# A fused attention, gated feed-forward and routed-expert kernel: more weight conversion beside attention, a smaller conversion allowance afterwards

## The chip, the cores and the metric

One core of a Trainium2 chip runs the whole program in one launch. The metric is the device time of one execution in microseconds (us); lower is better. The engines are called PE (TensorE, matrix products), DVE (VectorE), ACT (ScalarE), POOL (GpSimd) and SP (SyncE, which issues nearly all DMAs here). Each engine works through its own instructions in the order in which they were written and waits at semaphores where it needs another engine.

## The reference, cut to what matters

Three layers follow one another on 2304 tokens of width 512:

```python
# 1. attention: batch 4, heads 8, 576 positions, head width 64, window of 64 positions
attn = softmax(mask(q @ k.T / 8));  x = attn @ v            # x: 2304 x 512
# 2. gated feed-forward, width 1536
xn = x / sqrt(mean(x * x) + 1e-6) * rms_g
x2 = (silu(xn @ w_gate) * (xn @ w_val)) @ w_out
# 3. eight experts, width 1024, one for each token
e = argmax(x2 @ wg);  out = prob[e] * (relu(x2 @ w1[e]) @ w2[e])
```

The weights of layer 2 arrive as 64-bit floats and are turned into 32-bit floats on the chip ("conversion"). The products of layers 2 and 3 are each made of three products of split operands: a number is split into a high part h and the rest l, and h·h, h·l and l·h are added.

## The kernel before, in words

**Attention** goes in 48 groups (loop at L499, group g). A group computes scores (PE), softmax (DVE L205, ACT L209), normalisation (DVE L217, POOL L218), transposes (PE L223), their copy out of PSUM (DVE L227), the product with v (PE) and the copy of the result (L245 on ACT or DVE in turn, L246 on ACT). The steps of one group are spread over six passes of the loop: transposes come 4 passes after the scores (LT), the product with v and its output 5 (LV). `guard(g)` (L213) adds 1e-9 to the row sums. Five passes after the last group (g = 48 to 52) drain it, and PE fills them with the first unit of layer 2.

**Side work in attention.** Other work is written as generators that yield a nominal price in us for DVE's time, and `Task` and `beside` (L251 to L285) hand it out. `attending_work(g)` (L468) runs in each pass between `normalise` and `softmax`; it has a credit that grows by CREDIT per pass, is capped at 1.0 and may go negative. It offers, in this order, `early_splits`, `norm(0)` (from pass 17), `norm(1)` (from pass 30) and, until a given number of steps is converted, `conversion`. A task that yields "rest" (it waits for ACT) is passed over until 1.2 of other work is handed out or the call ends; one that yields "step" is passed over until the next call. If all tasks rest, the call ends and what is left of its allowance is lost, but for a carry of at most 0.5 (1.0 in attention, credit and carry together).

**Conversion** of one of the 12 steps (a step is 128 of the 1536 columns) is two halves, each with a load of 768 KB (`w_load`, SP), a Square on ACT (L426) and four DVE instructions (L401, L406, L409, L416) at the nominal prices 0.55, 1.0, 1.0 and 0.9: 6.9 for a step. `norm(i)` normalises a sub-block of 384 tokens: it loads x, squares it (POOL for i < 2, else ACT L329), adds the squares (three DVE adds L334), sums over the partitions with a PE product on a bank lent by the caller, takes 1/sqrt by three Newton steps (ACT L352, DVE L354, DVE L356), and scales and splits (L363, ACT L365, L368). From i = 2 on its prices add up to 10.0: 1.5 for the adds, 0.9 for L344 and L346, 3.6 for Newton, 4.0 for scaling and splitting.

**Layer 2** goes in 72 units (loop at L843). A unit is one step for one sub-block: 24 gate and value products (`gate_val`), then `silu` (ACT L594, DVE L595 and L596, ACT L597, L598), and 9 output products (`out_b`), which PE makes one unit later. Units 0 to 3 are steps 0 and 1 for sub-blocks 0 and 1; units 4 to 23 are steps 2 to 11, each for sub-blocks 0 and 1; block 1 (units 24 to 47) takes sub-blocks 2 and 3 in turn, so that unit 24 needs norm 2 and unit 25 norm 3. In blocks 0 and 1 gate and value products use PSUM banks 0 and 1 in each unit but unit 1, so a unit's first product waits for the L595 of the unit before.

A unit's allowance for side work is `BUDGET[n] + min(spare, 0.5)`, less what splits and evacuations cost (1.2 for the gate and value weights of a step, every second unit); a debt is carried in full. The order is norm 1, conversion, the other norms (`normer`), routing. Two things are forced whatever the allowance: a step is converted three units ahead of its first use (L888), and before the next unit the norm that it needs is finished (L890 to L893):

```python
        budget = BUDGET[n] + min(spare, 0.5)
        budget -= sum(c for c, _ in rest)
        spare = beside([norm1, conv] + bg, budget)          # bg: norm1, normer, routes
        if u + 3 in heads:
            spare -= convert(max(f for _, f, _ in steps[:heads[u + 3] + 1]) + 1, conv)
        if u + 1 < len(units):
            while normed[0] < units[u + 1][1]:
                late = normer if norm1.done else norm1
                late.piece(bk if late.want == "bank" else None)
```

There is one `xr` buffer for all norms from i = 2 on, so norm 3 cannot load before norm 2 has made its last split.

Of the kernel before, what the change touches and what calls it, by code (L numbers as in the profile page):

```python
# [8 lines left out]
F32 = mybir.dt.float32  # L9
# [4 lines left out]
ALU = mybir.AluOpType  # L14
# [12 lines left out]
P = 128  # L27
# [8 lines left out]
SUB = 384  # L36
# [4 lines left out]

LT, LV = 4, 5
NQK = 3
G_LOAD, G_CONV, G_NORM = 8, 14, (12 + LV, 25 + LV)
CREDIT = 0.5, 0.8
BUDGET = [4.8, 3.4, 4.7, 4.7]


@with_exitstack
def attention_moe_moe_kernel(ctx, tc, qT, kT, vw, w1p, rms_g, wg2, wg2T, w2p, out):  # L50
    nc = tc.nc
# [9 lines left out]

    bank = [psum.tile([P, 512], F32, name=f"bank{i}") for i in range(8)]

    for i in range(2):

        nc.vector.memset(bank[i][:, SUB:], 0.0)
    ident = const.tile([P, P], F32, name="ident")
# [35 lines left out]
    wraw_t = [wr_p.tile([P, 2 * WB], F32, name=f"wraw{i}") for i in range(NF // 2)]  # L103
    wraw = [t[:, i * WB:(i + 1) * WB] for t in wraw_t for i in range(2)]
# [24 lines left out]
    wh_t, wl_t = {}, {}  # L129

    def place(k, key, what):

        p = next((p for p in places[key] if p[2] == what), None)
        here = p is not None
        if not here:
            p = min(places[key], key=lambda p: p[3])
        p[2:] = what, k
        wh_t[k, key], wl_t[k, key] = p[:2]
        return here
# [3 lines left out]
    f_p = pool("fill", 1, actx)  # L143
# [17 lines left out]
    a_s = pool("a_s", 3, actx)  # L161

    qz = [f_p.tile([P, P, NBLK], F32, name=f"qz{i}") for i in range(NQK)]
    for q in qz:
        for h in range(2):
            nc.vector.memset(q[64 * h:64 * h + 64, 64 * (1 - h):64 * (1 - h) + 64], 0.0)

    NU = B * NHP
    NG = NU * 3
    q_t, k_t, v_t, xo_t, p_t, pt_t, rs_t = {}, {}, {}, {}, {}, {}, {}  # L170

    def qk_load(u):
        if u < NU:
            b, hp = divmod(u, NHP)
# [10 lines left out]
    def v_load(u):  # L185
        if u < NU:
            b, hp = divmod(u, NHP)
            t, i = (wraw_t[3], u % 4) if u % 4 < 3 else (wraw_t[1], 2)
            v_t[u] = t[:, i * 8 * P:(i + 1) * 8 * P].rearrange("p (w c) -> p w c", c=P)
            nc.sync.dma_start(v_t[u], vw[b, hp])  # L190

    def scores(g):
# [17 lines left out]
                                 accum_out=rs[:, j:j + 1])  # L210

    def guard(g):
        nc.vector.tensor_scalar_add(rs_t[g], rs_t[g], 1e-9)  # L213

    def normalise(g):
        p, rs = p_t[g], rs_t.pop(g)
# [6 lines left out]
            nc.tensor.transpose(bank[3 + g % 2][:, j * P:(j + 1) * P], p[:, j], ident)  # L223

    def pt_copy(g):
        pt = pt_t[g] = wraw_t[1][:, (g % 5) * 3 * P:(g % 5 + 1) * 3 * P]
        nc.vector.tensor_copy(pt, bank[3 + g % 2][:, 0:3 * P])  # L227

    def pv(g):
# [7 lines left out]
    def xo_out(g):  # L237
        u, i0 = g // 3, 3 * (g % 3)
        b, hp = divmod(u, NHP)
        if g % 3 == 0:  # L240
            xo_t[u] = wraw_t[4 + u % 2][:, 4 * 512:4 * 512 + S]
        vb = bank[5 + g % 3][:, 0:3 * P].rearrange("p (j c) -> p j c", j=3)
        xo = xo_t[u]
        x3 = xo.rearrange("p (i c) -> p i c", c=64)
        (nc.scalar.copy if g % 2 else nc.vector.tensor_copy)(x3[0:64, i0:i0 + 3], vb[0:64, :, 0:64])  # L245
        nc.scalar.copy(x3[64:128, i0:i0 + 3], vb[64:128, :, 64:128])  # L246
        if g % 3 == 2:
            nc.sync.dma_start(xdram[b][hp], xo)
# [189 lines left out]
    converted, attending = [0], [True]  # L438
# [14 lines left out]

    def early_splits():

        yield lambda: converted[0] > 0
        place(0, "a", ("b", 0))
        wh, wl = wh_t[0, "a"], wl_t[0, "a"]
        for a in range(0, 1024, 512):
            src, h = wraw[0][:, a:a + 512], slice(a, a + 512)  # L460
            nc.scalar.copy(wh[:, h], src)
            nc.gpsimd.tensor_tensor(out=wl[:, h], in0=src, in1=wh[:, h].bitcast(F32), op=ALU.subtract)
            yield "step"

    conv, early, norm0, norm1, normer = (Task(t) for t in (conversion(), early_splits(), norm(0), norm(1), norms()))
    credit = [0.0]
# [1 line left out]
    def attending_work(g):  # L468
        c = min(credit[0] + CREDIT[g >= G_NORM[1]], 1.0)
        if g >= G_CONV:  # L470
            tasks = [early]
            if g >= G_NORM[0]:
                tasks.append(norm0)
            if g >= G_NORM[1]:
                tasks.append(norm1)
            if converted[0] < 2:
                tasks.append(conv)
            tasks = [t for t in tasks if not t.done]
            c -= on_bank(tasks, bank[(g + 1) % 3 if g < NG else 2])
            c = beside(tasks, c)  # L480
        credit[0] = c
# [100 lines left out]
    def gate_val(u):  # L582
        if u > 0:
            for _ in gate_val_mm(gv_banks(u), *units[u]):
                pass
# [257 lines left out]
    for u, (k, i) in enumerate(units):  # L843
        n = steps[k][0]
        first, last = (i == steps[k][2][x] for x in (0, -1))
        begin = u == starts[blocks[n][2][0]]
        gate_val(u)
        if u == 0:
            beside([norm1, conv], 3.0)
        silu(u)  # L850
        budget = BUDGET[n] + min(spare, 0.5)

        if len(blocks[n][2]) > 1:
            bk = bank[1]
        else:
            bk = bank[4] if n == len(blocks) - 1 else bank[5]
        if u > 0:
            out_b(u - 1)
        if not (begin and len(blocks[n][2]) == 1):
            budget -= on_bank(bg, bk)  # L860
        if u > 0:
            budget -= evac(u - 1)
        if u == stops[i]:
            free[0] = i + 1
        if u in range(2, 2 + 2 * E, 2):

            e = u // 2 - 1
            nc.sync.dma_start(xs[e * NT:e * NT + 4 * P], x2dram[NT:NT + 1].to_broadcast([4 * P, DM]))
        rest = b_split(heads[u + 1], "o") if u + 1 in heads else []
        if u + 2 in heads:  # L870
            rest += b_split(heads[u + 2], "a")
        elif u + 2 >= len(units):
            rest += c_split(u + 2 - len(units), True)
        if conv.done and wg_bc is None:
            right.close()
            g_p, r_p, j_p = (pool(x, b, right, side="right") for x, b in (("g", 1), ("r", 2), ("j", 2)))
            wg_bc = g_p.tile([P, E, DM], F32, name="wg_bc")
            nc.sync.dma_start(wg_bc, wg2T.partition_broadcast(P))
        budget -= sum(c for c, _ in rest)
        spare = beside([norm1, conv] + bg, budget)  # L880
        for _, r in rest:
            r()
        if n == len(blocks) - 1 and last:

            while c_next < NRING and (c_next + 1) * W2B <= (NF + 2 + k - len(steps)) * WB:
                c_load(c_next)
                c_next += 1
# [6 lines that stand above are left out]
        bg = [t for t in bg if not t.done]  # L894
# [178 lines left out]
    with tc.If(n_over > 0):  # L1073
        with tc.For_i(0, n_over, 1) as i:
            ex = nc.values_load(slot[0:1, bass.ds(i, 1)], engines=(ET.SP,), min_val=0, max_val=E - 1)
            row = nc.values_load(slot[0:1, bass.ds(i + NS, 1)], engines=(ET.SP,), min_val=0, max_val=E * NT - 2 * P)
            with tc.tile_pool(name="ovr", bufs=1) as o_p:
                ix = o_p.tile([P, 2, 2], I32, name="oix")
                nc.sync.dma_start(ix, table[bass.ds(row, 2 * P)].rearrange("(j p) w -> p j w", p=P))
                w = o_p.tile([P, NF2, W2B], F32, name="ow")  # L1080
# [4 lines left out]
                for j in range(2):  # L1085
                    nc.gpsimd.indirect_dma_start(
                        out=xg[:, j], out_offset=None, in_=x2dram[:, :],
# [64 lines left out]
```

## Time and profile before

| | |
|---|---|
| timed runs | 901.14 us median of 3 (900.82 to 901.97) |
| the profiled execution | 898.3 us, of which the span from first to last instruction is 896.5 |
| PE, DVE, ACT, POOL busy | 94%, 74%, 46%, 23% of the span |
| mean granted TensorE clock | 0.986 of 2.4 GHz |

Times inside the profile are us from the start of the span. Busy shares are means over stages with different limits: attention lasts until about 130 us, block 0 of layer 2 until about 300, block 1 until about 450. A timeline row has start, duration, engine, line, operation, output and input, how many instructions were merged and, in brackets, the idle time of that engine just before and what ended it. A row of busy time by stretch has the stretch, its length, the busy us (and instructions) of PE, of PE's weight loads, of DVE, ACT and POOL, then PE's granted clock as a share of 2.4 GHz, the DMA engines' busy share and GB/s.

### The profile page before, as it was taken

The numbers are of one execution on the slowest core, as the hardware profiler recorded it, in microseconds if no ns is written. First come the engines' busy times: TensorE is split into PE (matmuls) and PEld (weight loads), VectorE is DVE, ScalarE is ACT, GpSimd is POOL, SyncE is SP. The second block draws the span as 40 slices with busy tenths as digits, with TensorE's granted clock in tenths as the row PEclk, the third lists the DMA queues.
The fourth block names the chain that finished last, engine by engine and source line by source line (L and its number), as shares of the span: only waits on it lengthen the run. The fifth ranks groups of instructions, "written<-read, shape, count | busy, mean of one in ns | idle before, by whom it ended". The sixth has DMA issues, their size and how long they took to land.

```text
span 896.5 us, 13576 instructions
## 1 busy us (share of the span) xinstructions
PE 844.1 (94%) x4667; PEld 774.7 (86%) x4667; DVE 665.6 (74%) x1552; ACT 415.3 (46%) x951; POOL 205.6 (23%) x226
## 2 busy tenths in 40 slices
PE   7999978998999999999999999997999999989995
PEld 7999977887888899999989999986888888878884
DVE  6789979999997677777578985696685765666453
ACT  5777764333443334323233333343564554555352
POOL 3347563323233100001400024003310120121011
PEclk9999998999999999999999999998999999999998
DMA  7988524779742301000120004634385664662010
GB/s 210 296 270 284 166 94 132 222 184 192 220 114 95 106 0 36 1 1 1 60 83 1 1 13 119 256 120 118 105 278 186 215 216 133 210 213 94 3 44 19
DMA packets 47071, 114.49 MB, mean 128 GB/s; under 512 B 10223, under 2 KB 14703, under 8 KB 46834
## 3 DMA queue, kind: packets, MB, share of 16 engines
q1 hardware_dynamic: 42386, 103.50, 38.1%
q0 software_dynamic: 4576, 9.47, 3.1%
q8 instruction: 77, 1.26, 0.6%
q14 instruction: 32, 0.26, 0.1%
HBM read 93.90 MB, written 31.10 MB: 139 GB/s over the span
## 4 chain that ended last, share of the span: by engine, by line
PE 55%; DVE 28%; issue 8%; DMA 4%; ACT 3%; POOL 2%; SPq 0%; DVEq 0%; POOLq 0%; ACTq 0%
PE bank L56 52%; DVE junk L661 4%; DVE wla L552 3%; DMA out_dram<-x,ix 3%; DVE wraw L406 3%; DVE wraw L409 2%; DVE wraw L416 2%; DVE t L596 2%; DVE t L595 2%; DVE wraw L401 2%; PE bank L796 1%; PE bank L223 1%; DVE xt L368 1%; DVE wlo L552 1%; ACT hh L597 1%
## 5 line engine op out<-in xcount | busy, mean ns | idle before, releaser
L56 PE MATMUL bank<-xt,wha 128*128 128x384 f32 (+3 forms) x1728 | 422.6, 329 | 24.6 <-DVE t L595 12.8
L56 PEld LDWEIGHTS bank<-xt,wha 128*128 128x128 f32 x1728 | 305.6, 190 | 43.1 <-DVE t L595 18.2
L56 PE MATMUL bank<-xt,wla 128*128 128x384 f32 (+3 forms) x864 | 282.0, 326 | 3.7 <-POOL wla L552 2.7
L56 PEld LDWEIGHTS bank<-xt,wla 128*128 128x128 f32 x864 | 164.1, 190 | 6.0 <-POOL wla L552 3.0
L56 PE MATMUL bank<-who,hl 128*128 128x512 f32 x384 | 152.5, 397 | 0.6 <-DVE hl L955 0.6
L56 PE MATMUL bank<-wlo,hh 128*128 128x512 f32 x384 | 152.4, 397 | 0.0
L56 PE MATMUL bank<-who,hh 128*128 128x512 f32 x384 | 151.5, 395 | 0.3
L597 ACT CAST hh<-t 128x384 fp32r<-128x384 f32 x72 | 37.0, 513 | 200.6 <-DVE t L596 200.6
L955 DVE SCALAR_TENSOR_TENSOR hl<-bank,hh 128x512 fp32r<-128x512 f32 (+1 forms) x72 | 45.3, 629 | 80.3 <-ACT hh L954 77.2
L552 DVE TENSOR_TENSOR wla<-wraw,wha 128x512 fp32r<-128x512 f32 (+1 forms) x112 | 98.0, 875 | 4.4 <-ACT wha L550 2.8
L56 PEld LDWEIGHTS bank<-who,hl 128*128 128x128 f32 x384 | 72.6, 189 | 17.4 <-DVE hl L955 1.4
L550 ACT CAST wha<-wraw 128x512 fp32r<-128x512 f32 (+1 forms) x113 | 87.1, 771 | 0.0
L954 ACT ACTIVATE hh<-bank 128x512 fp32r<-128x512 f32 (+1 forms) x72 | 39.7, 551 | 99.6 <-PE bank L56 99.3
L971 POOL DMA_INDIRECT out_dram<-x,ix x32 | 34.9, 1091 | 214.3 <-ACT x L970 207.3
L56 PEld LDWEIGHTS bank<-who,hh 128*128 128x128 f32 x384 | 72.8, 190 | 11.8 <-issue 0.5
L56 PEld LDWEIGHTS bank<-wlo,hh 128*128 128x128 f32 x384 | 72.8, 190 | 11.1
L56 PE MATMUL bank<-kt,qz 128*128 128x128 f32 x288 | 76.2, 404 | 5.5 <-DMA kt<-in_kT_dram 4.8
L550 ACT CAST who<-wraw 128x512 fp32r<-128x512 f32 x111 | 68.7, 619 | 21.9 <-PE bank L56 19.6
L56 PEld LDWEIGHTS bank<-kt,qz 128*128 128x128 f32 x288 | 72.3, 333 | 6.1 <-issue 4.8
L552 DVE TENSOR_TENSOR wlo<-wraw,who 128x512 fp32r<-128x512 f32 x99 | 68.1, 688 | 12.4 <-ACT who L550 5.7
L661 DVE SCALAR_TENSOR_TENSOR junk<-x,wg_bc 128x512 f32<-128x512 f32 x120 | 76.1, 687 | 0.0
L209 ACT ACTIVATE wraw<-sm,nm 128x128 f32<-128x128 f32 x144 | 56.2, 391 | 25.9 <-DVE nm L205 25.4
(151 smaller groups left out, 974.5 us busy)
## 6 DMA issues: line engine op xcount, KB each, us to landing
wraw<-in_w2p_dram SPq DMA_DIRECT2D x64, 512.0 KB
st<-in_w1p_dram SPq DMA_DIRECT2D x24, 768.0 KB
wraw<-in_vw_dram SPq DMA_DIRECT2D x16, 512.0 KB
xs<-x2dram SPq DMA_DIRECT2D x8, 1024.0 KB
qz<-in_qT_dram SPq DMA_DIRECT2D x32, 144.0 KB
xdram<-wraw SPq DMA_DIRECT2D x16, 288.0 KB
x2dram<-x SPq DMA_DIRECT2D x18, 256.0 KB
kt<-in_kT_dram SPq DMA_DIRECT2D x15, 288.0 KB
```

Source lines behind the costliest of these rows:

```text
L56: nc.tensor.matmul(o, l, r, start=start, stop=stop)
L209: nc.scalar.activation(p[:, j], sm[:, j], AF.Exp, bias=nm[:, j:j + 1], scale=-1.0, accum_out=rs[:, j:j + 1])
L401: nc.vector.tensor_scalar(out=w, in0=hi, scalar1=3, scalar2=0x3FFFFFFF, op0=ALU.logical_shift_left, op1=ALU.bitwise_and)
L406: nc.vector.scalar_tensor_tensor(out=w, in0=lo, scalar=29, in1=w, op0=ALU.logical_shift_right, op1=ALU.bitwise_or)
L409: nc.vector.scalar_tensor_tensor(out=w, in0=hi, scalar=-0x40000000, in1=w, op0=ALU.bitwise_and, op1=ALU.bitwise_or)
L550: nc.scalar.copy(wh, src[:, r])
L552: e.tensor_tensor(out=wl, in0=src[:, r], in1=wh.bitcast(F32), op=ALU.subtract)))
L597: nc.scalar.copy(hh[:, :nt], t)
L661: nc.vector.scalar_tensor_tensor(out=junk, in0=x2, scalar=1.0, in1=wg_bc[:, e], op0=ALU.mult, op1=ALU.mult, accum_out=lg[:, j, e:e + 1])
L954: nc.scalar.activation(hh[:, :n], bank[k % 2][:, :n], AF.Relu, scale=1.0)
L955: nc.vector.scalar_tensor_tensor(out=hl[:, :n], in0=bank[k % 2][:, :n], scalar=0.0, in1=hh[:, :n].bitcast(F32), op0=ALU.max, op1=ALU.subtract)
L971: d = nc.gpsimd.indirect_dma_start(out=out[:, :], in_=y, in_offset=None, out_offset=bass.IndirectOffsetOnAxis(ap=ix[:, j, 0:1], axis=0), b ...
```

## The change

- Loads for conversion start at groups 3, 5, 7 instead of 8, 10, 12; conversion beside attention starts in pass 6 instead of 14 and goes on until four steps are converted instead of two; the credit for each pass is 0.85 instead of 0.5 (later 0.8).
- `early_splits` splits the gate and value weights of steps 0 and 1, not of step 0 alone (ACT and POOL).
- Steps 2 and 3 live in a tile that held v for every fourth head pair and the transposed probabilities. These get tiles of their own: `v3`, and `pt` from a pool of three.
- `guard` becomes an instruction with a second input in PSUM that is zero, so a third bank's tail is set to zero at the start. All output copies of attention run on ACT.
- The allowance of a unit of block 0 is 3.8 instead of 4.8.
- The `silu` of unit 0 comes ahead of the first call of `beside`.

```diff
-G_LOAD, G_CONV, G_NORM = 8, 14, (12 + LV, 25 + LV)
-CREDIT = 0.5, 0.8
-BUDGET = [4.8, 3.4, 4.7, 4.7]
+G_LOAD, G_CONV, G_NORM = 3, 6, (12 + LV, 25 + LV)
+EARLY = 4
+CREDIT = 0.85, 0.85
+BUDGET = [3.8, 3.4, 4.7, 4.7]
...
-    for i in range(2):
+    for i in range(3):
         nc.vector.memset(bank[i][:, SUB:], 0.0)
...
+    v3 = f_p.tile([P, 8 * P], F32, name="v3")
...
-            t, i = (wraw_t[3], u % 4) if u % 4 < 3 else (wraw_t[1], 2)
+            t = wraw_t[3][:, u % 4 * 8 * P:(u % 4 + 1) * 8 * P] if u % 4 < 3 else v3
...
     def guard(g):
-        nc.vector.tensor_scalar_add(rs_t[g], rs_t[g], 1e-9)
+        nc.vector.scalar_tensor_tensor(out=rs_t[g], in0=rs_t[g], scalar=1e-9, in1=bank[(g + 1) % 3][:, SUB:SUB + 3],
+                                       op0=ALU.add, op1=ALU.add)
...
-        pt = pt_t[g] = wraw_t[1][:, (g % 5) * 3 * P:(g % 5 + 1) * 3 * P]
+        pt = pt_t[g] = a_s.tile([P, 3 * P], F32, name="pt")
...
-        (nc.scalar.copy if g % 2 else nc.vector.tensor_copy)(x3[0:64, i0:i0 + 3], vb[0:64, :, 0:64])
+        nc.scalar.copy(x3[0:64, i0:i0 + 3], vb[0:64, :, 0:64])
...
     def early_splits():
-        yield lambda: converted[0] > 0
-        place(0, "a", ("b", 0))
...
+        for k in range(2):
+            yield lambda: converted[0] > k
+            place(k, "a", ("b", k))
...
-            if converted[0] < 2:
+            if converted[0] < EARLY:
                 tasks.append(conv)
...
         gate_val(u)
+        silu(u)
         if u == 0:
             beside([norm1, conv], 3.0)
-        silu(u)
```

## Rows read from the trace of the kernel before

**Rows 1.** Busy time by stretch (start:end us); columns as told under the table above.

```profile
20.00:40.00 20.00, 20.00 (x124) 20.00 (x124) 14.49 (x77) 13.83 (x58) 6.71 (x8) 1.00 0.85 272
...
100.00:120.00 20.00, 19.60 (x124) 19.41 (x125) 19.34 (x92) 17.58 (x72) 15.44 (x16) 1.00 0.44 136
...
138.00:140.00 2.00, 2.00 (x8) 2.00 (x8) 1.27 (x3) 0.36 (x2) 0.00 (x0) 0.50 0.05 19
...
181.19:194.79 13.60, 12.81 (x66) 11.68 (x66) 13.22 (x17) 5.38 (x9) 4.28 (x3) 1.00 0.81 192
...
328.73:431.00 102.27, 102.27 (x538) 95.55 (x537) 76.00 (x175) 33.07 (x60) 2.28 (x6) 1.00 0.03 8
```

**Rows 2.** Timeline of DVE in attention.

```profile
37.31 1.47 DVE L406 SCALAR_TENSOR_TENSOR wraw<-st,wraw 128x768 int32<-128x768 int32 x1
...
62.93 0.56 DVE L227 COPY wraw<-bank 128x384 f32<-128x384 f32 x1 [0.77 <-PE bank L223]
...
65.37 0.56 DVE L227 COPY wraw<-bank 128x384 f32<-128x384 f32 x1 [0.77 <-PE bank L223]
```

**Rows 3.** Timeline of PE from the end of attention to unit 3.

```profile
129.37 0.83 PE L56 MATMUL bank<-wraw 128*128 128x128 f32 x6
132.97 0.61 PE L56 MATMUL bank<-xt,wha 128*128 128x384 f32 x2 [2.77 <-ACT wha L550]
136.30 0.69 PE L56 MATMUL bank<-xt,wla 128*128 128x384 f32 x1 [2.72 <-POOL wla L552]
...
144.48 0.51 PE L56 MATMUL bank<-xt,wha 128*128 128x384 f32 x2
...
148.67 0.39 PE L56 MATMUL bank<-who,hh 128*128 128x512 f32 x1
...
152.93 0.62 PE L56 MATMUL bank<-xt,wha 128*128 128x384 f32 x2 [1.98 <-DVE t L595]
```

**Rows 4.** Timeline of PE: first output product made in units 22, 23, 25.

```profile
290.27 0.39 PE L56 MATMUL bank<-who,hh 128*128 128x512 f32 x1
...
296.54 0.39 PE L56 MATMUL bank<-who,hh 128*128 128x512 f32 x1
...
309.10 0.39 PE L56 MATMUL bank<-who,hh 128*128 128x512 f32 x1
```

**Rows 5.** Costliest groups, conversion on DVE: busy us, mean ns of one, idle before.

```profile
L406 DVE SCALAR_TENSOR_TENSOR wraw<-st,wraw 128x768 int32<-128x768 int32 x24 | 29.7, 1240 | 0.8
L409 DVE SCALAR_TENSOR_TENSOR wraw<-st,wraw 128x768 int32<-128x768 int32 x24 | 29.4, 1224 | 0.7
...
L416 DVE SCALAR_TENSOR_TENSOR wraw<-gt,wraw 128x768 f32<-128x768 f32 x24 | 23.8, 992 | 0.2
...
L401 DVE TENSOR_SCALAR wraw<-st 128x768 int32<-128x768 int32 x24 | 21.4, 894 | 0.0
```

**Rows 6.** Line 213, the guard: ns shortest/median/longest, first and last start.

```profile
L213 DVE TENSOR_SCALAR rs<-rs x48: 148/222/1042, 8.7 to 124.3; 128x3 f32<-128x3 f32 x48
```

**Rows 7.** Timeline of DVE: norm 3 in unit 22, norm 4 in units 24 and 25.

```profile
290.94 0.55 DVE L354 TENSOR_TENSOR sq<-sq 128x384 f32<-128x384 f32 x1
...
292.12 1.78 DVE L363 SCALAR_TENSOR_TENSOR xr<-xr,gs_sb,sq 128x384 f32<-128x384 f32 x2
...
296.73 0.56 DVE L368 TENSOR_TENSOR xt<-xr,xt 128x384 fp32r<-128x384 f32 x1 [0.17 <-ACT xt L365]
...
304.88 0.56 DVE L596 SCALAR_TENSOR_TENSOR t<-t,bank 128x384 f32<-128x384 f32 x1
...
308.62 0.68 DVE L661 SCALAR_TENSOR_TENSOR junk<-x,wg_bc 128x512 f32<-128x512 f32 x1
...
312.71 0.55 DVE L344 TENSOR_SCALAR sq<-bank 128x384 f32<-128x384 f32 x1
```

**Rows 8.** Timeline of ACT: a Newton square of norm 3, the squares of norm 4.

```profile
285.86 0.53 ACT L352 ACTIVATE sq<-sq 128x384 f32<-128x384 f32 x1
...
302.05 1.77 ACT L329 ACTIVATE sq<-xr 128x384 f32<-128x384 f32 x4 [2.11 <-DMA xr<-xdram]
```

More of the change, by code (lines that the diff above doesn't have):

```diff
@@ L187, in v_load @@
             b, hp = divmod(u, NHP)
-            t, i = (wraw_t[3], u % 4) if u % 4 < 3 else (wraw_t[1], 2)
-            v_t[u] = t[:, i * 8 * P:(i + 1) * 8 * P].rearrange("p (w c) -> p w c", c=P)
+            t = wraw_t[3][:, u % 4 * 8 * P:(u % 4 + 1) * 8 * P] if u % 4 < 3 else v3
+            v_t[u] = t.rearrange("p (w c) -> p w c", c=P)
             nc.sync.dma_start(v_t[u], vw[b, hp])
@@ L454, in early_splits @@
     def early_splits():
-        yield lambda: converted[0] > 0
-        place(0, "a", ("b", 0))
[L458 to L463, printed above, removed]
+        for k in range(2):
+            yield lambda: converted[0] > k
+            place(k, "a", ("b", k))
+            wh, wl = wh_t[k, "a"], wl_t[k, "a"]
+            for a in range(0, 1024, 512):
+                src, h = wraw[k][:, a:a + 512], slice(a, a + 512)
+                nc.scalar.copy(wh[:, h], src)
+                nc.gpsimd.tensor_tensor(out=wl[:, h], in0=src, in1=wh[:, h].bitcast(F32), op=ALU.subtract)
+                yield "step"
     conv, early, norm0, norm1, normer = (Task(t) for t in (conversion(), early_splits(), norm(0), norm(1), norms()))
```

## The prediction, made before the change was run

> **What bounds the kernel now.** I read the stretches first, then PE's timeline where PE is not full, then what it waits for. In attention PE is full and DVE is not: in the stretch from 20 us DVE works 14.49 of 20, in the one from 100 us 19.34 [rows 1]. A group takes 2.44 us, and in it DVE sits 0.77 idle until PE's transposes are made [rows 2]. From the end of attention (129.37 + 0.83 = 130.2) to unit 3 PE is held up three times, by ACT's and POOL's split of step 1 (2.77 and 2.72) and by L595 (1.98) [rows 3], and after the idle time it runs at a granted clock of 0.50, 1.2 GHz, for some us [rows 1]. In block 0 two units take 13.60, in which DVE works 13.22 and PE 12.81 [rows 1]: DVE's queue sets the pace, since a unit's first product waits for L595 and L595 stands behind conversions. PE alone would need 296.54 − 290.27 = 6.27 for a unit [rows 4], 12.54 for two. In block 1 PE is full for 102 us with DVE at 76 [rows 1]: what is lost ahead of that stretch is not caught up there.
>
> So DVE's work is free in attention and dear in block 0. What block 0 could give back is this. Unit 3's gate and value products start at 152.93 and take 148.67 − 144.48 = 4.19 [rows 3], so they end at 157.1; those of unit 23 end at 296.54, where the output products begin [rows 4]. These 139.4 us hold 20 units, 125.4 at PE's pace, and two norm products of some 0.8: 12.4 are lost to DVE.
>
> **The change, part by part.**
>
> *Attention.* A conversion step is 8 DVE instructions, 2 × (0.89 + 1.24 + 1.22 + 0.99) = 8.7 [rows 5]; two more steps are 17.4. A group's DVE work is 2.44 − 0.77 = 1.67 [rows 2]; with a credit of 0.85 it becomes 2.52, 0.08 over the group. Against that DVE loses half of the output copies (to ACT, busy 17.58 of 20 at its fullest [rows 1]) and guard gets shorter: it took 0.222 in the median, 0.148 at the least [rows 6]. The new guard reads PSUM, which no row here shows for that shape; I bound it by 0.15 and 0.22. So DVE has as much time as it needs, within 0.1 a group; the cover is the 0.77, and if it misses by 0.1 in the 42 passes with conversion, attention is 4 longer. I take 0 (bounds 0 and 4). The 47 × 0.85 = 40 of credit stand against 27.6 (four steps), 6.5 (norm 0) and 8.5 (norm 1): the fourth step's last piece and norm 1's scaling stay for after it. The earlier loads put two transfers of 768 KB ahead of one v and one q and k on SP's queue; at the 272 GB/s of [rows 1] that delays them by 6 once, and they are issued some 6 groups (14.6) before use: nothing. If that cover were gone it would cost 6. POOL's extra split, the third memset and the new buffers I count at nothing: the transposes are consumed one pass after `pt` is written, so three buffers do, and POOL is idle for most of attention. Norm 1's product moves from the drain into attention; that is even.
>
> *Handover.* Without waits, from 130.2, PE would make gate(1), out(0), gate(2), out(1), gate(3) in 3 × 4.19 + 2 × 2.09 = 16.8; it takes 26.9 [rows 3], 10.1 lost. Steps 0 and 1 being split beforehand removes 5.5 of it and with it the half clock (four eighths of a gate at double time, 1.8). Late next: norm 1's scaling still follows attention on DVE, now behind the moved `silu(0)` (whose POOL subtraction also comes ahead of step 1's output split), so gate(2) is fed as it goes (2.2), and `silu(1)` comes after it and 2.5 of conversion, so out(1) waits (2.3). I expect 4.5 lost, a gain of 5.6 (bounds 2 and 9).
>
> *Block 0.* Eight steps are left instead of ten. The allowance of two units is 7.6 less 1.2 for the split, 6.4; a step costs 6.9. So conversion, first in the order, still takes nearly all of it, and the pace is kept by the forced conversions. I went through the hand-out piece by piece from the code (for the kernel before the same walk puts norm 3's last split in unit 22 and norm 4's squares in unit 23, where [rows 7, 8] have them). After: steps 4 to 7 are converted in units 0 to 11, evenly. From unit 12 the debt holds the even units empty, and the odd units 13, 15, 17, 19 convert up to two halves at once, 8.7 [rows 5]. A unit loses nothing while its side work fits into 6.27 + 2.09 − 1.2 (L595, L596) = 7.2, so units 15 to 19 lose about 1.2 each, 3.7 together, and 1.0 for odds and ends: block 0 to unit 23 takes 125.4 + 0.8 + 4.7 = 130.9 instead of 139.4, a gain of 8.5 (bounds 2, if DVE goes on setting the pace from unit 8, and 11.6, if nothing waits).
>
> *The norms.* This is where it is given back. Units 0 to 23 hand out 24 × 3.8 = 91.2, less 10 splits and one evacuation, 12.6: 78.6. Asked for are 4.1 (norm 1), 55.2 (eight steps), 10 (norm 2) and 10 (norm 3): 79.3, too little even if nothing is lost while tasks rest. Before it was 102.6 for 5.2 + 69 + 20 = 94.2. In my walk conversion ends in unit 19, norm 2 in unit 22, norm 3 loads then, squares in unit 23 and adds in unit 24; all the rest of it (8.5 of 10) is forced at the end of unit 24, and unit 25 needs it.
>
> Let T be the end of unit 23's gate products. Norm 3's load starts where norm 4's starts now or 2 earlier (297.29, that is 296.73 + 0.56, T + 0.75), lands 4.8 later (squares at 302.05) [rows 7, 8], which is ahead of `silu(24)`. L596 of unit 24 starts at T + 6.3, and the adds end 308.62 − 304.88 = 3.7 later [rows 7]: T + 10.0. PE has run dry at T + 8.4 (out(22), gate(24), out(23)). Product, L344 (0.55) and L346: 2.0 [rows 7]. Three Newton steps, 0.55 for ACT and 292.12 − 290.94 = 1.18 for DVE each [rows 7, 8]: 5.2, T + 17.2. Scaling and splitting took 297.29 − 292.12 = 5.2 with POOL splitting beside it [rows 7]; I take 4.6, T + 21.8. Gate(25) follows the splits, ends its first half 0.5 later and its second 2.09 after that: T + 24.4. Now it ends at T + 12.56 [rows 4]. That is 11.8, and 0.8 for a clock that has fallen in the wait (0 to 2): 12.6 lost (bounds 9 and 14).
>
> **The sum.** 0 − 5.6 − 8.5 + 12.6 = −1.5, so a span of 895.0 and a profiled execution of 896.8 against 898.3. The runs' median lies 2.8 above the profiled execution; I keep that: 901.14 − 1.5, say 899.6.
>
> **Rivals.**
>
> *A. Norm 2 slips by a unit, and it is slower.* Norm 2 ends in unit 22 with 3.6 of allowance for six pieces priced 3.0. If the debt is 0.6 more there, its last split falls into unit 23, norm 3's load starts after it, T + 1 at the earliest with squares forced in unit 24, and all of the chain moves by up to a unit, 6.27: 905.9. For it: the debt is carried in full. Against: the walk met each place of the kernel before. 0.23, with 903 to 909.
>
> *B. Norm 3 is not in the way.* If the forced pieces ran beside PE's work, only the gains would stay: 901.1 − 14.1 = 887. For it: DVE has 2.4 spare in each even unit. Against: an engine runs its queue in order, and the pieces are written behind unit 24's. 0.14, with 884 to 893.
>
> *C. Conversion collides with POOL in attention.* One L406 beside POOL's normalisation took 1.47 [rows 2], 0.48 over the 0.99 of L416's mean [rows 5]. If the side work of every pass paid that, a group would be 1.67 + 0.85 + 0.48 = 3.00, 0.56 over its time, and 42 passes 23 longer: 923. Against: the mean of L406 itself is 1.24, and the stretch from 100 us, at a credit of 0.8 and with POOL at 15.4 of 20, still has PE at 19.6 [rows 1]. 0.04. The Trainium skill (SBUF — State Buffer, Who interferes with whom) has a rule for it: a VectorE instruction with two SBUF inputs and a GpSimd instruction that reads SBUF take a shared port as an exclusive lock, and the later one waits for all of the other. By that rule three of the four conversion instructions, added beside 48 normalisations, speak against the change; the trace agrees that single ones wait, but not that the pass as a whole does.
>
> *D. It does not do what it says*, the credit being lost to resting tasks so that three steps are converted at the end of attention: unit 0 then starts 6.9 behind, and norm 2 slips as in A. It is in A's chance.
>
> **How the numbers follow.** Forecast 0.55, with its own range 896 to 903 (the bounds of handover, block 0 and norms do not add up all at one end); A 0.23, B 0.14, C 0.04; 0.04 lies between B and the forecast. The likeliest is 899.6. From 889 to 907 leaves out half of B, C and the far end of A, together 0.2. A difference under 0.2%, 1.8 us, cannot be told from none here: faster is below 899.3 and has B, the gap and half of the forecast, 0.46; slower, above 902.9, has A, C and the forecast's end, 0.29; the same 0.25.
>
> **What would show it.** Attention: PE full to about 130, DVE above 18 of 20 from 25 us on, groups of 2.44. Handover: gate(1) right behind the last product with v, no clock below 1.00 there, unit 3 done near 151.5. Block 0: two units in 12.5 to 12.6 up to unit 12, waits for L595 of 1 to 2 after units 15, 17, 19, unit 23 done near 282.4. Then PE idle for some 9 to 10 in two pieces, waiting for L334 and for L365 and L368, between out(23) and gate(25), and the same 6.27 a unit behind it. The prediction is wrong if that gap is short or absent, if groups of attention take 2.5 or more, or if block 0 stays at 13.6 for two units.

## The result, and the profile after

The changed kernel takes 906.94 us (median of 17 runs, 901.4 to 918.13), the kernel before 900.82 beside it (17 runs, 895.75 to 903.84): a ratio of 1.0062, with a 95% interval of 1.0043 to 1.0081. The run of 918.13 was in a slow state and does not count in the ratio. The change makes the kernel slower, by less than 1%; the forecast was 899.6, a little faster. The profiled execution took 906.26, span 904.1, against 898.3 and 896.5.

In the changed kernel L57 is L56 of before, L223 the normalisation L218, L228 the transposes L223, L339 the adds L334, L332 the squares L327 and L349 the L344 of a norm, L601 to L604 are L595 to L598, L370 and L373 L365 and L368, L468 the early split on POOL (L462), L411 the second instruction of conversion (L406), L212 the softmax on ACT (L209).

The stretches that answer to [rows 1]:

```profile
20.00:40.00 20.00, 20.00 (x124) 19.92 (x123) 18.72 (x84) 17.90 (x68) 11.79 (x10) 1.00 0.85 274
100.00:120.00 20.00, 17.73 (x104) 16.36 (x103) 17.35 (x72) 15.97 (x64) 19.79 (x19) 1.00 0.57 190
184.00:196.50 12.50, 12.50 (x68) 11.71 (x67) 12.00 (x16) 3.74 (x7) 1.98 (x2) 1.00 0.82 163
```

From 20 us DVE has been filled, as the change wants, with PE still full. After 40 us DVE works 16.7 to 17.6 of 20, under the 18 of the forecast: the shorter guard and the output copies moved to ACT give back 16 of the 19 us that two more steps cost DVE in attention. From 100 us PE has fallen from 19.60 to 17.73, and it is not DVE that is full (17.35) but POOL: 19.79 of 20, where it had 15.44. In block 0 PE is full for two units in 12.50, where it had 12.81 of 13.60.

PE's timeline: waits of attention, the handover, the end of block 0 and the gap (answers to [rows 3, 4]).

```profile
67.11 0.55 PE L228 MATMUL bank<-ident,wraw 128*128 128x128 f32 x3 [1.39 <-POOL wraw L223]
...
111.04 0.55 PE L228 MATMUL bank<-ident,wraw 128*128 128x128 f32 x3 [0.43 <-POOL wraw L223]
114.12 0.55 PE L228 MATMUL bank<-ident,wraw 128*128 128x128 f32 x3 [0.43 <-POOL wraw L223]
118.92 0.91 PE L57 MATMUL bank<-wraw,ones 128*128 128x384 f32 x2 [1.16 <-POOL wraw L339]
120.49 1.80 PE L57 MATMUL bank<-kt,qz 128*128 128x128 f32 x6 [0.65 <-DVE wraw L349]
...
134.55 0.83 PE L57 MATMUL bank<-pt,v 128*128 128x128 f32 x6
139.40 0.39 PE L57 MATMUL bank<-who,hh 128*128 128x512 f32 x1
140.57 0.50 PE L57 MATMUL bank<-who,hl 128*128 128x512 f32 x1 [0.54 <-POOL hl L604]
...
145.01 0.45 PE L57 MATMUL bank<-xt,wha 128*128 128x384 f32 x1 [0.78 <-DVE xt L373]
149.14 0.50 PE L57 MATMUL bank<-who,hh 128*128 128x512 f32 x1 [1.43 <-ACT hh L603]
...
156.16 0.39 PE L57 MATMUL bank<-who,hh 128*128 128x512 f32 x1
...
270.45 0.62 PE L57 MATMUL bank<-xt,wha 128*128 128x384 f32 x2 [1.76 <-DVE t L601]
...
288.82 0.39 PE L57 MATMUL bank<-who,hh 128*128 128x512 f32 x1
...
299.16 0.91 PE L57 MATMUL bank<-sq,ones 128*128 128x384 f32 x2 [1.82 <-DVE sq L339]
308.33 1.28 PE L57 MATMUL bank<-xt,wha 128*128 128x384 f32 x2 [8.26 <-ACT xt L370]
314.73 0.39 PE L57 MATMUL bank<-who,hh 128*128 128x512 f32 x1
```

Attention now ends at 134.55 + 0.83 = 135.38 instead of 130.2. Of the 4.9 that PE waits in it (1.9 before), 3.4 are for POOL's normalisation L223 and POOL's adds L339; the rest is for DVE's L349, which follows a norm's product. Gate(1) follows at once, without the 2.77 and 2.72 of [rows 3], and unit 3 is done at 156.16: the handover takes 20.8 instead of 27.0 (unit 3 was done at 157.20). The gate products of unit 23 end at 288.82, 132.7 later (139.3 before). Then PE stands for 1.82 and 8.26, and those of unit 25 end at 314.73, 25.9 after unit 23's, instead of 12.56.

POOL's timeline where PE loses most in attention:

```profile
103.18 3.96 POOL L373 TENSOR_TENSOR xt<-xr,xt 128x384 fp32r<-128x384 f32 x3
107.09 0.82 POOL L223 TENSOR_TENSOR wraw<-wraw,rs 128x384 f32<-128x384 f32 x1
107.88 2.32 POOL L332 TENSOR_TENSOR wraw<-wraw 128x384 f32<-128x384 f32 x2
110.17 0.82 POOL L223 TENSOR_TENSOR wraw<-wraw,rs 128x384 f32<-128x384 f32 x1
110.95 1.61 POOL L332 TENSOR_TENSOR wraw<-wraw 128x384 f32<-128x384 f32 x2
112.52 2.64 POOL L223 TENSOR_TENSOR wraw<-wraw,rs 128x384 f32<-128x384 f32 x2
115.12 3.75 POOL L339 TENSOR_TENSOR wraw<-wraw 128x384 f32<-128x384 f32 x3
118.83 1.61 POOL L223 TENSOR_TENSOR wraw<-wraw,rs 128x384 f32<-128x384 f32 x2
```

No row has an idle time in brackets: POOL works back to back, through norm 0's splits, norm 1's squares and its adds. Each normalisation stands behind a piece of a norm. At 112.52 and at 118.83 two of them run together, so one of each two is most of a pass late. The transposes wait for normalisations at 67.11, 111.04 and 114.12; at 118.92 PE waits for the adds.

Four stages, each read as above (us; end of the last product with v, then unit 3, units 4 to 23, and from unit 23 to unit 25, each to the end of its gate and value products):

| | attention ends | handover | units 4 to 23 | unit 23 to 25 | unit 25 at |
|---|---|---|---|---|---|
| before | 130.20 | 27.0 | 139.3 | 12.56 | 309.10 |
| forecast, as differences | 0 | -5.6 | -8.5 | +12.6 | -1.5 |
| changed kernel | 135.38 | 20.8 | 132.7 | 25.91 | 314.73 |
| measured differences | +5.2 | -6.2 | -6.7 | +13.35 | +5.63 |

The span is 7.6 longer, 2.0 more than the +5.63 at unit 25. The change touches no line that runs there (its last 460 products took 98.4 at a mean granted clock of 0.94, before 96.0 at 0.96), and over the ten executions profiled for this document, with all experiments, what follows unit 25 took between 585.6 and 593.2. So stages of two profiles can be compared up to unit 25, and their spans only within some 8 us.

The medians differ by 6.1, about what stands at unit 25. Two smaller answers. The guard takes 0.15, the lower of the two bounds from [rows 6]. And the second of the conversion's instructions has become a little longer in attention (from 10 to 131 us, the kernel before first); its mean over the whole program fell from 1.24 [rows 5] to 1.09, which says nothing of this stage:

```profile
L406 DVE SCALAR_TENSOR_TENSOR wraw<-st,wraw 128x768 int32<-128x768 int32 x4 | 4.8, 1193 | 0.1
L411 DVE SCALAR_TENSOR_TENSOR wraw<-st,wraw 128x768 int32<-128x768 int32 x8 | 9.9, 1236 | 0.1
```

### The profile page after: what moved, and what is told of

Its sections match the earlier page's. It is cut to its first block, busy times and chain, and to the rows that moved or that the text cites. A ratio compares the mean times of both kernels' runs of the same rounds, so it can differ in the third digit from the quotient of the medians.

```text
span 904.1 us, 13559 instructions
## 1 busy us (share of the span) xinstructions
PE 847.0 (94%) x4667; PEld 777.0 (86%) x4667; DVE 649.5 (72%) x1529; ACT 424.3 (47%) x976; POOL 208.9 (23%) x227
## 4 chain that ended last, share of the span: by engine, by line
PE 66%; DVE 18%; issue 7%; DMA 4%; ACT 3%; POOL 1%; SPq 0%; DVEq 0%; POOLq 0%; ACTq 0%
PE bank L57 63%; DVE junk L667 4%; DMA out_dram<-x,ix 3%; DVE wla L558 2%; DVE t L602 1%; PE bank L228 1%; DVE wraw L414 1%; DVE wraw L421 1%; DVE t L601 1%; PE bank L802 1%; DVE wlo L558 1%; DMA st<-in_w1p_dram 1%; ACT hh L603 1%; DVE wraw L411 1%; DVE hl L604 1%
## 5 line engine op out<-in xcount | busy, mean ns | idle before, releaser
L57 PE MATMUL bank<-xt,wha 128*128 128x384 f32 (+3 forms) x1728 | 424.1, 330 | 25.5 <-ACT xt L370 8.3
L57 PEld LDWEIGHTS bank<-xt,wha 128*128 128x128 f32 x1728 | 307.2, 191 | 43.5 <-ACT xt L370 8.9
L57 PE MATMUL bank<-xt,wla 128*128 128x384 f32 (+3 forms) x864 | 282.6, 327 | 1.0 <-DVE wla L558 1.0
L57 PEld LDWEIGHTS bank<-xt,wla 128*128 128x128 f32 x864 | 164.9, 191 | 3.0 <-DVE wla L558 2.4
L57 PE MATMUL bank<-who,hl 128*128 128x512 f32 x384 | 152.1, 396 | 1.7 <-POOL hl L604 0.9
L57 PE MATMUL bank<-who,hh 128*128 128x512 f32 x384 | 151.5, 395 | 1.7 <-ACT hh L603 1.4
L57 PE MATMUL bank<-wlo,hh 128*128 128x512 f32 x384 | 152.0, 396 | 0.0
L57 PEld LDWEIGHTS bank<-who,hl 128*128 128x128 f32 x384 | 72.4, 188 | 18.9 <-POOL hl L604 1.8
L57 PEld LDWEIGHTS bank<-who,hh 128*128 128x128 f32 x384 | 72.9, 190 | 13.5 <-ACT hh L603 1.7
L57 PEld LDWEIGHTS bank<-wlo,hh 128*128 128x128 f32 x384 | 72.8, 190 | 11.1
L57 PE MATMUL bank<-kt,qz 128*128 128x128 f32 x288 | 76.2, 406 | 6.2 <-DMA kt<-in_kT_dram 4.8
L57 PEld LDWEIGHTS bank<-kt,qz 128*128 128x128 f32 x288 | 72.3, 333 | 7.4 <-issue 4.7
L556 ACT CAST who<-wraw 128x512 fp32r<-128x512 f32 x111 | 68.7, 619 | 19.6 <-PE bank L57 16.6
L710 POOL TENSOR_TENSOR tot<-tot,ohb 128x8 f32<-128x8 f32 x18 | 5.5, 307 | 288.4 <-DVE gw L697 287.3
```

The source lines that it names most:

```text
L57: nc.tensor.matmul(o, l, r, start=start, stop=stop)
L556: nc.scalar.copy(wh, src[:, r])
```

## The experiments

My theory after the comparison: the lower allowance starves norm 3 (13 lost, as forecast), and POOL's queue, not DVE, makes attention 5 longer (not forecast). The rival to both is that DVE's sum of work is the bound wherever it is put.

### 1. Allowance back at 4.8

```diff
-BUDGET = [3.8, 3.4, 4.7, 4.7]
+BUDGET = [4.8, 3.4, 4.7, 4.7]
```

> The changed kernel with the allowance of block 0 back at 4.8; all else as changed. Theory (the cut of the allowance starves the norms, and norm 3's chain is forced in front of unit 25): conversion ends in unit 17 and norm 3 in unit 22, PE waits 1 or less before unit 25 instead of 8.3 + 1.8, attention and handover as in the changed kernel (unit 3 done near 156), units 3 to 23 need 132 to 136 (132.7 in the changed kernel), so 12 to 13 less than the changed kernel: 893 to 896, ratio to the kernel before 0.991 to 0.996. Rival (DVE's sheer amount of work, whatever the order, is the bound): the gap before unit 25 goes but comes back as 13.6 for two units all through block 0, and the time stays at 904 to 908.

900.15 us, ratio to the kernel before 0.9995 (0.9963 to 1.0028). The gap is gone: unit 23 ends at 296.65 and unit 25 at 309.18, 12.53 later.

```profile
296.65 0.39 PE L57 MATMUL bank<-who,hh 128*128 128x512 f32 x1
...
309.18 0.39 PE L57 MATMUL bank<-who,hh 128*128 128x512 f32 x1
```

But units 4 to 23 take 137.7, not 132 to 136; PE waits 8.1 for L601 in seven of them (4.2 in three in the changed kernel). So the theory holds for the gap, and the rival for about five of the thirteen: what the norms take out of the gap they put back into the units. Another 2.8 are lost ahead of unit 4 (unit 3 is done at 158.92): attention ends 1.4 later than in the changed kernel, with a late first load (run 3) and a lower granted clock from 66 to 72 us, and the handover takes 1.3 longer, 0.99 of it a wait for L601. The time is 4 above the expected range and 4 below the rival's.

### 2. Squares of norms 0 and 1 on ACT

```diff
-            if i < 2:
-                nc.gpsimd.tensor_tensor(out=sq[:, c, :nt], in0=xr[:, c, :nt], in1=xr[:, c, :nt], op=ALU.mult)
-            else:
-                nc.scalar.activation(sq[:, c, :nt], xr[:, c, :nt], AF.Square, scale=1.0)
+            nc.scalar.activation(sq[:, c, :nt], xr[:, c, :nt], AF.Square, scale=1.0)
```

> The changed kernel with the eight squares of norms 0 and 1 made on ACT instead of POOL; the order of everything else as changed. Theory (attention is 5 longer because POOL's queue jams: early splits, norm squares, adds and norm 0's splits ahead of the normalisations that the transposes wait for): POOL loses 8 squares of 0.8 to 1.2, about half of the excess, so the last product with v ends at 131.5 to 133 instead of 135.1, and the time falls by 2 to 4 to 903 to 905. Rival 1 (DVE is over-filled by the conversions): attention ends at 135 as before and the time does not move. Rival 2 (ACT, busy 18 to 19 of 20 at its fullest, becomes the bound): attention ends at 136 or later.

904.65 us, ratio 1.0042 (1.0011 to 1.0073), as expected; attention ends at 131.16 + 0.83 = 131.99, 3.4 earlier than in the changed kernel. Some 1.1 of the 3.4 is TensorE's clock, which did not fall here at 122 us; against that, a later first load costs 0.8 (run 3). The edit makes the kernel three lines shorter, so L336 is L339, L346 L349, and L598 to L601 are L601 to L604, here and in runs 5 and 6. The stretch from 100 us, and what PE waits for in all of attention (line waited for: us, times, longest):

```profile
100.00:120.00 20.00, 18.60 (x111) 17.60 (x110) 17.75 (x76) 18.66 (x73) 16.29 (x15) 1.00 0.65 217
```

```profile
PE bank L57 <- DVE sq L346: 1.0, 1, 1.0
PE bank L57 <- ACT wraw L212: 0.7, 1, 0.7
PE bank L57 <- DVE wraw L346: 0.7, 1, 0.7
PE bank L57 <- POOL wraw L336: 0.6, 1, 0.6
```

No wait for L223 is left (2.2 in three waits in the changed kernel). DVE has the same pieces to do and is busier in that stretch (17.75 against 17.35), so DVE was not what held attention up; POOL's queue was.

### 3. Step 0 alone split in attention

```diff
-        for k in range(2):
+        for k in range(1):
```

> The changed kernel with the gate and value weights of step 0 alone split in attention; step 1 is split after it, as in the kernel before. Theory (POOL's queue): the stretch from 58 to 68 loses two POOL instructions of 1.3 to 1.6 and so most of its 2.0 of lost time, attention ends near 133; then gate(1) waits for ACT's and POOL's split of step 1, 2.8 + 2.7 as in the kernel before, with a lower clock after it, unit 3 ends at 158 to 160 instead of 156.2, and the time is 2 to 4 longer, 909 to 911. Rival (the second split is not in POOL's way): attention ends at 135 and the time is 5 to 7 longer, 912 to 914.

907.23 us, ratio 1.0061 (1.0035 to 1.0088). The profiled execution was the slowest of the ten (912.72), by what follows unit 25. Unit 3 is done at 159.70, as the theory has it; attention ends at 135.74, as the rival has it. The rows say why both. DVE's and PE's timelines in the first passes:

```profile
19.97 0.56 DVE L406 TENSOR_SCALAR wraw<-st 128x768 int32<-128x768 int32 x1 [2.61 <-DMA st<-in_w1p_dram]
```

```profile
22.79 1.23 PE L57 MATMUL bank<-pt,wraw 128*128 128x128 f32 x6 [1.25 <-ACT wraw L212]
...
138.12 0.62 PE L57 MATMUL bank<-xt,wha 128*128 128x384 f32 x2 [2.38 <-ACT wha L556]
140.84 0.69 PE L57 MATMUL bank<-xt,wla 128*128 128x384 f32 x1 [2.10 <-POOL wla L558]
```

The wait of 1.39 at 67 us is gone: waits for L223 fall from 2.2 to 0.8, so the second split was part of the jam. In its place something came that has nothing to do with the edit. The first conversion stands in DVE's queue in pass 6, ahead of that pass's softmax, and its load of 768 KB landed at 19.97 here, 2.61 after DVE had got there. The same wait is 1.22 in the changed kernel's profile, 1.77 in run 1 and 2.00 in run 2: it costs attention 0.1 in the first of these and 0.6 to 2.4 in the others. Less the 2.4 it costs here, attention would end at 133.3, where the theory had it. So splitting step 1 early costs about 2.0 in attention and is worth 24.0 - 20.8 = 3.2 in the handover.

### 4. The kernel before with an allowance of 3.8

```diff
-BUDGET = [4.8, 3.4, 4.7, 4.7]
+BUDGET = [3.8, 3.4, 4.7, 4.7]
```

> The kernel before with one thing changed, block 0's allowance of 3.8. Theory (the allowance feeds the norms last, so cutting it starves them while the conversions are forced at the same pace): units 4 to 20 keep about 13.6 for two, norm 2 is finished by force at the end of unit 23 and the whole of norm 3, load and squares included, at the end of unit 24, so PE waits 5 to 10 before unit 24 and 15 to 22 before unit 25: 918 to 930. Rival (a lower allowance takes work off DVE's queue where PE waits): two units of block 0 in 12.6 and a time of 890 to 901.

930.2 us, ratio 1.0313 (1.0266 to 1.0361), 0.2 above the theory's range.

```profile
307.22 1.28 PE L56 MATMUL bank<-xt,wha 128*128 128x384 f32 x2 [5.95 <-ACT xt L365]
...
321.02 1.65 PE L56 MATMUL bank<-sq,ones 128*128 128x384 f32 x2 [4.88 <-DVE sq L334]
330.19 1.28 PE L56 MATMUL bank<-xt,wha 128*128 128x384 f32 x2 [7.52 <-ACT xt L365]
```

Units 24 and 25 wait for norms 2 and 3, 5.95 and 4.88 + 7.52, and units 4 to 23 take 141.9: with ten steps the conversions are forced at the old pace, so the cut saves nothing at all (139.3 before). Before unit 25 PE waits 12.4, less than the 15 to 22 expected. In the changed kernel, where eight steps are left, the same cut saves 5.1 in units 4 to 23 and loses 13.4 behind them (run 1).

### 5. Three repairs together

Allowance 4.8, squares on ACT, and the first conversion in pass 7.

```diff
-G_LOAD, G_CONV, G_NORM = 3, 6, (12 + LV, 25 + LV)
+G_LOAD, G_CONV, G_NORM = 3, 7, (12 + LV, 25 + LV)
-BUDGET = [3.8, 3.4, 4.7, 4.7]
+BUDGET = [4.8, 3.4, 4.7, 4.7]
```

> The changed kernel with the three repairs that the first four runs point to: allowance 4.8, the squares of norms 0 and 1 on ACT, and the first conversion in pass 7 instead of 6 (its load lands 0.6 to 2.6 after DVE and ACT get to it in pass 6). Theory (each of the three is a separate loss): the kernel with allowance 4.8 took 900.15; attention gives back 3 to 4, the late load 0 to 1.5, norm 1 loses up to 1.2 because 0.85 of credit is gone: 895 to 897.5, ratio to the kernel before 0.994 to 0.997, the last scores starting near 120. Rival (what attention gives back is lost again in block 0, where DVE sets the pace and unit 23 ends when DVE's work is through, whenever unit 4 began): 899 to 901.

895.97 us, ratio 0.9946 (0.9927 to 0.9965): faster than both kernels, as the theory of separate losses has it. Attention ends at 131.77 without a wait for the first load, the handover takes 22.7, units 4 to 23 137.7 as in run 1.

### 6. The norms ahead of conversion

As run 5, with an allowance of 4.6 and:

```diff
-        spare = beside([norm1, conv] + bg, budget)
+        ranked = [norm1, normer, conv] if u >= 4 else [norm1, conv, normer]
+        spare = beside(ranked + [t for t in bg if t not in ranked], budget)
```

> The same repairs with an allowance of 4.6, and from unit 4 on norms 2 and 3 come ahead of conversion in the order of side work (conversion still forced three units ahead of its use). Theory (block 0's losses come from the order and the unevenness of DVE's side work, not from its sum: with an allowance of 4.8 a unit with conversion and norm pieces holds 6 to 6.6 of DVE work beside its own 1.2, a unit after conversion has ended 1 to 2): norm 2 done in unit 7, norm 3 in unit 22, conversion spread over units 0 to 19 at 4.5 to 5.6 a unit, units 3 to 23 in 130 to 134 instead of 137.7, no gap before unit 25: 889 to 893, ratio 0.988 to 0.992. Rival (DVE's sum of work is the bound, so order changes nothing): 895 to 897.5, as with conversion first. Rival 2 (forced conversions of odd units hold PE up more than the early norms save): above 898.

894.27 us, ratio 0.9929 (0.9903 to 0.9955), between the theory and its rival. PE's waits from unit 4 to unit 25, here and then in run 5:

```profile
PE bank L57 <- DVE t L598: 3.0, 6, 0.8
PE bank L57 <- DVE t L599: 2.6, 2, 1.4
```

```profile
PE bank L57 <- DVE t L598: 6.8, 6, 1.8
PE bank L57 <- DVE t L599: 0.8, 1, 0.8
```

Units 4 to 23 take 135.0, 2.7 less than in run 5. Not all of that is the order: in run 5 the granted clock stood at 0.50 from 222 to 225 us, behind the wait of 1.8, and that unit took 9.94, where it took 8.38 in run 1 behind an equal wait at a clock of 1.00; in run 6 the clock did not fall in block 0. That leaves about 1.1 for the order and for the lower allowance, which were changed together. The time is 1 to 5 short of the expectation: the waits for L598 are halved, but norm 2's and norm 3's products now wait 1.4 and 1.2 for L599. The times of runs 5 and 6 alone, with overlapping intervals, would not tell them apart.

### 7. The first silu moved back

```diff
         gate_val(u)
-        silu(u)
         if u == 0:
             beside([norm1, conv], 3.0)
+        silu(u)
```

> The changed kernel with the first silu back behind the first call of side work. Theory of the prediction (silu(0) ahead feeds out(0), and norm 1 ahead feeds gate(2)): out(0) waits some 3 for L602 and POOL's hl instead of 0.5, gate(2) no longer waits 0.8, so unit 3 is done 1.5 to 2.5 later after the end of attention (22.5 to 23.5 instead of 21.0), and the time is 1 to 3 longer than the changed kernel's: 908 to 910. Rival (the order of the two makes no difference, since PE needs both before gate(3)): 21.0 again and 905.5 to 908.

905.03 us, ratio 1.0052 (1.0033 to 1.007); the handover takes 20.55, against 20.78. The rival was right (its range began 0.5 higher). PE's two main waits there:

```profile
142.57 0.50 PE L57 MATMUL bank<-who,hh 128*128 128x512 f32 x1 [2.45 <-ACT hh L603]
143.88 0.50 PE L57 MATMUL bank<-who,hl 128*128 128x512 f32 x1 [0.58 <-POOL hl L604]
```

Out(0) waits 3.0 here and out(1) 0.2; in the changed kernel out(0), gate(2) and out(1) wait 0.54 + 0.78 + 1.43 and 0.36. The sums are nearly the same, 3.2 and 3.1, which fits the rival's reason: DVE has both pieces of work to do before gate(3).

### 8. The kernel before with the handover's parts alone

The loop of two early splits and the moved silu of the change, all else as before.

> The kernel before with two parts of the change alone: gate and value weights of step 1 split in attention too, and the first silu moved up; two steps converted beside attention, all else as before. Theory (the handover's gain stands by itself; it was eaten by attention and the norms): gate(1) follows the last product with v, the second split meets norm 1's adds on POOL in the last passes and costs 0 to 2 there, unit 3 ends at 152.5 to 154.5 instead of 157.1; block 0 at DVE's pace keeps 1 to 3 of it: 897 to 899.5. Rival (block 0's end is set by DVE's work alone, so an earlier unit 3 gives nothing at unit 23): 900 to 901.5. Rival 2 (the second split in the last passes delays the end of attention by its whole 2.6 to 3.2): unit 3 ends at 156 or later, 899 to 901.

902.09 us, ratio 1.0015 (0.9993 to 1.0037): no gain, and 1.1 above the ranges of both rivals. By its stages it is rival 2. Unit 3 is done at 156.54, 0.7 earlier than before, and attention ends at 132.44, 2.2 later. POOL's and PE's timelines in the last passes:

```profile
118.31 1.27 POOL L463 TENSOR_TENSOR wla<-wraw,wha 128x512 fp32r<-128x512 f32 x1
119.53 0.83 POOL L218 TENSOR_TENSOR wraw<-wraw,rs 128x384 f32<-128x384 f32 x1
120.32 1.27 POOL L463 TENSOR_TENSOR wla<-wraw,wha 128x512 fp32r<-128x512 f32 x1
121.55 3.03 POOL L334 TENSOR_TENSOR wraw<-wraw 128x384 f32<-128x384 f32 x3
```

```profile
120.42 0.55 PE L223 MATMUL bank<-ident,wraw 128*128 128x128 f32 x3 [1.63 <-DVE rs L213]
...
124.64 0.91 PE L56 MATMUL bank<-wraw,ones 128*128 128x384 f32 x2 [1.93 <-POOL wraw L334]
```

The profile names DVE for the wait of 1.63, but the reciprocal that follows L213 was done at 118.9; the transposes begin at 120.42, just behind the normalisation that ends at 119.53 + 0.83 = 120.36. It is POOL again: the second split, of which each half takes 1.27, stands ahead of a normalisation and of norm 1's adds. Of the 2.9 that the handover saves (24.1 for 27.0), 2.2 are paid in the passes before it. At unit 25 this execution is 1.0 ahead of the kernel before (308.09 for 309.10), too little to show in the medians.

## Why the prediction was wrong

**The step that failed** is in *Attention*: "I take 0 (bounds 0 and 4)", and in it the sentence that counts "POOL's extra split" at nothing because "POOL is idle for most of attention". Measured: +5.2, above the upper bound too. That premise was wrong for the kernel before already: [rows 1] have POOL at work for 15.44 of 20 us at the end, and all of attention but its ends for 58.29 of 100:

```profile
20.00:120.00 100.00, 98.81 (x608) 97.81 (x608) 87.07 (x414) 78.19 (x315) 58.29 (x58) 1.00 0.74 236
```

I had weighed DVE, whose time is what the change spends, and that weighing held: PE is full from 20 to 40 us with DVE at 18.72. I had not laid out POOL's queue pass by pass. With more credit the handing-out also brings the norms' pieces closer together: norm 0's splits, norm 1's squares and its adds fell between 101 and 119 us (98 to 122 before), 12.6 of POOL's time beside seven normalisations that took 7.0: 19.6 in seven passes of 2.44, which are 17.1. The mean busy share of POOL, 23% in both kernels, hides it. From 10 to 131 us POOL works 9.8 more than before, and half of that is no new work. The second split is 2.7 of it; the same 48 normalisations, now beside twice as many conversions, take 5.1 more (before, after):

```profile
L218 POOL TENSOR_TENSOR wraw<-wraw,rs 128x384 f32<-128x384 f32 x48 | 47.1, 983 | 54.2 <-DVE rs L217 37.5 <-ACT wraw L209 13.3 <-ACT wraw L246 3.4
L223 POOL TENSOR_TENSOR wraw<-wraw,rs 128x384 f32<-128x384 f32 x48 | 52.2, 1091 | 48.1 <-DVE rs L222 34.2 <-ACT wraw L212 7.8 <-DVE wraw L406 1.6
```

Runs 2 and 3 show the cause from both sides: without the squares the waits for L223 are gone and attention ends 3.4 earlier; without the second split the one at 67 us is gone. Run 8 shows the same jam in the kernel before with the second split added. Of the rest, 1.1 is TensorE at a granted clock of 0.50, 1.2 GHz, from 122 to 124 us, behind the waits of 1.16 and 0.65. Rival C had the right place and in part the right cause, conversions and POOL slowing each other, but it priced the wrong engine: half a conversion step, four instructions, grew from 3.98 to 4.41 on DVE in attention, 3.4 over its eight halves, while the normalisations grew by 5.1 on POOL and got late behind the norms' pieces. Its 23 is far from the 5.2.

The step also passed over the first conversion's own load: the 6 "once" that I reckoned for v, q and k did not show, but 0.1 to 2.4 for `st` did (run 3), and pass 7 cures it (runs 5 and 6).

**Block 0** was right in kind and 1.8 off in size: waits for L601 came where the walk through the code had them, three of 0.99, 1.41 and 1.76 (1.2 each was forecast). The term that was too small is "1.0 for odds and ends": behind the wait of 1.76 the clock stood at 0.50 from 272 to 275 us, half a gate's time lost. In runs 2 and 3, where the clock did not fall behind that wait, the same units took 131.1, 0.2 over the forecast. (The upper bound of the gain, 11.6, does not follow from its own terms: 139.4 less 125.4 and 0.8 is 13.2. The result rests on neither.)

**The norms** were right: forced at the end of unit 24, as forecast, 25.9 from unit 23 to unit 25 against 24.4 + 0.8, so a loss of 13.35 for 12.6. Rival A did not come about, norm 2 ending in unit 22; that its 905.9 lies near the result is chance. Rival B is excluded by the 8.26.

**The handover** gave 6.2 for 5.6, but not by the steps that I named. The second split is worth 3.2 (run 3), where I had 5.5 and 1.8 of clock, since behind those two waits the others of the handover (3.1 in the changed kernel) are gone; moving the silu is worth nothing (run 7). The other 3.0 show in run 3, which splits step 1 late as the kernel before does: its waits for that split are 1.0 shorter (2.38 and 2.10), and the wait of 1.98 for L595 before gate(3) is gone. At an allowance of 4.8 half of that last wait is back (0.99, run 1), so the lower allowance has a part in it; what else has was not tested.

So +5.2 in place of 0 turns -1.5 into +3.7, and block 0, 1.8 dearer, the norms, 0.8 dearer, and the handover, 0.6 cheaper, make it +5.6. That the change as a whole is not bad is shown by runs 5 and 6: its conversions and splits, with the norms fed and POOL relieved, are 4.9 and 6.6 faster than the kernel before in the medians. In run 6 block 0 still loses 135.0 less 125.4 (20 units at 6.27) less 1.6 (two norm products): 8.0. What of it is DVE's sum of work and what its order stays open.

## What to carry to other kernels

Before work is pushed into a stage because one engine has room, lay out the queues of all engines there pass by pass: an engine that is busy for a quarter of the span can be full for 20 us, and what stands in its queue behind the new work is late. Count also how much longer its old instructions take beside the new work of another engine. When an allowance is cut, ask who is last in the order, for it loses all of the cut, and if it is forced later it comes as one gap. And a part of a change whose gain the trace shows (here the second split, 3.2) can be paid for in large part by what it displaces one stage earlier (here about 2.0), so read it from the stage's start to the next stage's end.

## What the runs showed of the hardware

POOL's normalisation takes 0.83 alone and 1.36 to 1.39 where one of DVE's two-input conversions began just before it (L414 at 21.32 in the changed kernel, the normalisation at 21.55). The other way round, L411 took 1.91 where POOL's split had begun first (59.67 and 60.16), 0.96 alone. The conversion's one-input L406 took 0.56 alone and 1.19 beside a normalisation (25.54). Norm 1's three adds took 3.75 in the changed kernel and 3.04 before. The Trainium skill (SBUF — State Buffer, Who interferes with whom) says that a VectorE instruction with two SBUF inputs and a GpSimd instruction that reads SBUF contend for a shared port; the trace agrees for single instructions, on either side.

The same wait does not always cost the same clock. Behind L601's wait of 1.76 in the changed kernel the granted clock was 0.50 for 3 us; behind its twin of 1.75 in run 2 (the same instructions of the same unit) it stayed at 1.00. So it was for a wait of 1.8 in runs 5 and 1: 0.50 behind it in run 5, 1.00 in run 1. Here are the first of these stretches and the second:

```profile
272.00:275.00 3.00, 3.00 (x11) 3.00 (x10) 1.81 (x2) 1.04 (x2) 0.75 (x1) 0.50 1.01 431
```

```profile
269.00:272.00 3.00, 3.00 (x20) 3.00 (x19) 1.47 (x3) 1.96 (x3) 1.01 (x1) 1.00 1.01 421
```

And a load of 768 KB that is issued at the same place of the program landed between 18.6 and 20.0 us in five executions, which by itself moved the end of attention by up to 2.4.
